# Value and carried products 128 columns wide, in a gated linear attention with a mixture of experts

## The chip, the core and the metric

The kernel runs on one core of a Trainium2 chip. The metric is device time of one execution in microseconds (us); the figure for a kernel is the median of its runs. The engines are named TensorE (PE, matrix products; PEld is its loading of weights), VectorE (DVE), ScalarE (ACT), GpSimd (POOL) and SyncE (SP, which issues transfers). SBUF is the on-chip memory of 128 partitions, PSUM the memory of eight banks that TensorE writes.

## The reference

Two stages follow one another. The first is a recurrent attention over 4 batches, 8 heads, 768 positions and head width 40. A matrix state C and a vector state n are decayed by a forget gate and take in each position's value and key, in a form stabilized by a running maximum m:

```python
for t in range(S):
    m_new = np.maximum(f_gate[:, :, t] + m, i_gate[:, :, t])
    f_stab = np.exp(f_gate[:, :, t] + m - m_new)
    i_stab = np.exp(i_gate[:, :, t] - m_new)
    C = f_stab * C + i_stab * np.einsum('bhd,bhe->bhde', vt, kt)
    n = f_stab * n + i_stab * kt
    h_tilde = np.einsum('bhde,bhe->bhd', C, qt)
    denom = np.maximum(np.abs(np.einsum('bhd,bhd->bh', n, qt)), 1.0)
    y[:, :, t] = sigmoid(o_gate[:, :, t]) * h_tilde / denom
```

The second stage takes the 3072 resulting rows of 320 numbers, picks for each the best of 4 groups and in it the best of 4 experts, and replaces the row by `combined * relu(x @ w1) @ w2` of that expert (320 to 1024 to 320), weighted with the two softmax weights. All numbers are float32.

## The kernel before

The attention is computed in 24 units: 6 chunks of 128 positions, in each of them the 4 batches, one unit for all 8 heads of a batch (`u = 4 * chunk + batch`). Within a chunk the recurrence is a masked product: scores (k by q, line 203, tile `sp`) times decays (outer sums on TensorE, line 176, tile `aw`, exponentials on ScalarE, line 186, tile `ab`), and the product `pt` (line 208) times the values. The values (line 273, tile `av`) have a column of ones beside the 40 of a head, so each head's result is 41 columns wide (`D1`), the last being the denominator. All eight heads lie side by side in one PSUM bank. What earlier chunks carry comes from the state `Cst`: the carried product (line 227, tile `it`, from chunk 1 on), with the even heads in one bank and the odd ones in another, each again 41 wide. The unit's own contribution to the state (line 246) goes to the rest of the second of these banks.

On VectorE and GpSimd a unit is then finished: `carried2` scales the carried part, `norm1` adds it and computes the denominators, `rows` multiplies by the gate (line 290), `rows2` divides (GpSimd up to unit 19), `store` writes the rows to memory and `turn` transposes them on TensorE (line 301) for the routing logits. The gate itself is a tanh on ScalarE for a whole chunk (`gate_o`, line 154).

The order of work is written by hand up to unit 21: each engine executes its instructions in the order in which the code issues them, and waits at the first that isn't ready. `unit(u)` issues, for one unit, scores of u, the finishing steps of u - 1, masked scores and carried product of u, decays of u + 2, turn of u - 1, then values and state of u. Sums of the gates (`gate_sums`) are made for the first 128 positions, for the next 128, and for the remaining 512 in one piece, on VectorE, in steps that `sum_on` issues between units; the steps for the last 512 positions begin after unit 2. From unit 22 on, the scheduler of the language sets the order by readiness and priority. Weight loads and weight splits for the first expert are issued from units 14 to 21.

The experts follow: 16 of them in the order of their number of rows, each with a gather of its rows, a turn, two layers (lines 738 and 759 to 761, with float32 split into two parts; the last three experts use plain float32 in the first layer, line 706) and a scatter.

`busy` (line 119) issues products whose results nobody reads. Eleven of them stand at the kernel's start.

Of the kernel before, what the change touches and what calls it, by code (L numbers as in the profile page):

```python
# [7 lines left out]
F32 = mybir.dt.float32  # L8
# [4 lines left out]
ALU = mybir.AluOpType  # L13
# [5 lines left out]
P = 128  # L19
B, H, S, D = 4, 8, 768, 40  # L20
NCH = S // P
NU = NCH * B
DM = H * D
# [9 lines left out]
D1 = D + 1  # L33
HC = 4 * D1
# [18 lines left out]
def bc(ap, shape):  # L53
    return ap.broadcast_to(list(shape))
# [3 lines left out]
def lstm_moe(ctx: ExitStack, tc: tile.TileContext, gates, qkT, nat, og, wcat, w1, w2, cst, out):  # L58
    nc = tc.nc
    enter = ctx.enter_context  # L60
    mm = nc.tensor.matmul
# [38 lines left out]
    ap_ = att_pool("att", 1)  # L100
# [2 lines left out]
    Apc = ap_.tile([P, S], BF16, name="Apc")  # L103
    sel_b = ap_.tile([P, B * H], BF16, name="sel_b")
    decs = ap_.tile([P, NCH, B * 4], F32, name="decs")
    Cst = ap_.tile([P, B * 4, D1], F32, name="Cst")
    kws = [ap_.tile([P, H * D + 24], F32, name=f"kw{i}") for i in range(2)]
    bcol = ap_.tile([P, NCH, B * H], F32, name="bcol")
    eacol = ap_.tile([P, NCH, B * H], F32, name="eacol")
    wk = att_pool("wk", 2)  # L110
# [42 lines left out]
    def gate_o(c):  # L153
        nc.scalar.activation(sigs[c], sigs[c], AF.Tanh, scale=0.5)
# [33 lines left out]
    def decay(u, r, **kw):  # L188
        aprod(u, r, **kw)
        exps(u, r)  # L190
# [28 lines left out]
    def carried(u):  # L219
        c, b = divmod(u, B)  # L220
        t = st_[u]
        it = t["it"] = ps_a.tile([P, 2, 512], F32, name="it")
        if c > 0:
            for pr in range(4):
                for r in range(2):
                    rs = slice(64 * r, 64 * r + D)
                    mm(it[:, r, pr * D1:(pr + 1) * D1], t["qk"][rs, 1, pr, :], Cst[rs, b * 4 + pr, :], start=True, stop=True)  # L227

    def carried2(u):
        c, b = divmod(u, B)  # L230
        t = st_[u]
        if c > 0:
            num = t["num"] = wk.tile([P, H, D1], F32, name="num")
            nc.vector.tensor_tensor(num.rearrange("p (j r) e -> p r j e", r=2),
                                    t["it"][:, :, 0:HC].rearrange("p r (j e) -> p r j e", e=D1),
                                    bc(eacol[:, c, b * H:(b + 1) * H].rearrange("p (j r o) -> p r j o", r=2, o=1),
                                       (P, 2, 4, D1)), op=ALU.mult)

    def state(u):
        c, b = divmod(u, B)  # L240
        t = st_[u]
        nt = t["nt"]
        if c < NCH - 1:
            for j in range(H):
                pr, r0 = j // 2, 64 * (j % 2)
                mm(t["it"][r0:r0 + 64, 1, HC + pr * D1:HC + (pr + 1) * D1], t["kw"][:, j * D:j * D + 64],  # L246
                   nt[:, j * D1:(j + 1) * D1], start=True, stop=True)
# [18 lines left out]
    def values(u):  # L266
        c, b = divmod(u, B)
        t = st_[u]
        nt = t["nt"]
        av = t["av"] = ps_1.tile([P, 512], F32, name="av")  # L270
        for j in (0, 2, 4, 6, 1, 3, 5, 7):
            o = j * D1
            ins = mm(av[:, o:o + D1], t["pm"][j % 2][:, j // 2, :], nt[:, o:o + D1], start=True, stop=True)  # L273
        rt["av", u] = ins

    def norm1(u):
        num = st_[u]["av"][:, 0:H * D1].rearrange("p (h e) -> p h e", e=D1)
        if u >= B:
            nc.vector.tensor_tensor(num, num, st_[u]["num"], op=ALU.add)  # L279
        st_[u]["num"] = num  # L280
        den = st_[u]["den"] = wk.tile([P, H], F32, name="den")
        nc.vector.tensor_scalar(den, num[:, :, D], -2.0, 2.0, op0=ALU.mult, op1=ALU.max)
        nc.vector.scalar_tensor_tensor(den, num[:, :, D], 2.0, den, op0=ALU.mult, op1=ALU.max)
        nc.vector.reciprocal(den, den)

    def rows(u):
        c, b = divmod(u, B)
        num = st_[u]["num"]
        xn = st_[u]["xn"] = wk.tile([P, H, D], F32, name="xn")
        nc.vector.scalar_tensor_tensor(xn, sigs[c][:, b, :].rearrange("p (h d) -> p h d", d=D), 1.0, num[:, :, 0:D],  # L290
                                       op0=ALU.add, op1=ALU.mult)

    def rows2(u):
        x = wk.tile([P, 3 * P], F32, name="x", bufs=3)
        (nc.gpsimd if u < 20 else nc.vector).tensor_tensor(
            x[:, 0:DM].rearrange("p (h d) -> p h d", d=D), st_[u]["xn"], bc(st_[u]["den"].unsqueeze(2), (P, H, D)), op=ALU.mult)
        st_[u]["x"] = x

    def turned(tp, x, cols=(0, P, 2 * P)):
# [484 lines left out]
    def run(stage, u):  # L784
        if 0 <= u < NU:
            stage(u)
# [9 lines left out]
    xgs, early_loads, early_splits = {}, [], []  # L796
    MANUAL = 22

    def unit(u, more=0):
        run(loads, u + 3)  # L800
        if u == 6:
            first_tokens()
        if u == 9:
            last_rows()
        if u % B == 1 and u // B + 1 < NCH:
            load_o(u // B + 1)
        with ExitStack() as st:
            if u == MANUAL:
                st.enter_context(tc.issue_after(rt["av", u - 1].ins))
            run(scores, u)  # L810
        run(norm1, u - 1)
        run(rows, u - 1)
        run(state2, u - 1)
        run(rows2, u - 1)
        run(store, u - 1)
        run(mask, u + 1)
        run(lambda v: masked(v, 0), u)
        run(lambda v: masked(v, 1), u)
        run(carried, u)
        run(decayed, u)  # L820
        run(carried2, u)
        run(keyw, u + 1)
        run(lambda v: decay(v, 0), u + 2)
        run(turn, u - 1)
        if u % B == 1 and 1 < u < NU:
            logits_back(u // B - 1)
        go_on(9, "A")
        if u == 5:
            first_rows()
        if u > NU - 2:  # L830
            run(logits, u - 2)
        run(values, u)
        run(state, u)
        run(lambda v: decay(v, 1), u + 2)
        if u == 14:
            chores.append([first_experts(), "B"])
        if u == NU - 2:
            chores.append([early_counts(), "B"])
        if u < MANUAL:
            go_on(4 + more, "B")  # L840
        if u % B == 0 and 0 < u < NU:
            logits_of(u // B - 1)
        if u % B == 2 and u // B + 1 < NCH:
            gate_o(u // B + 1)
        for _ in range(1 if u < 20 else 3):
            put_id()
# [57 lines left out]
    with tc.manual_schedule():  # L904
        nc.sync.dma_start(G[:, :, 0:P], gates[:, :, 0:P])
        nc.scalar.dma_start(cs, cst)
        nc.scalar.dma_start(G[:, :, P:], gates[:, :, P:])
        nc.vector.memset(ones_b, 1.0)
        nc.vector.memset(sep, 0.0)
        nc.scalar.activation(sep, sep, AF.Exp)  # L910
        busy(11)
        nc.vector.memset(R_, 1.0)
        nc.vector.memset(R_.rearrange("h (c t) -> h c t", t=P)[:, :, 0:1], 0.0)
        nc.vector.memset(Dl[:, 0:1], 0.0)
        nc.vector.memset(Apc[96:P], 0.0)
        load_qk(0)
        loads(0)
        load_o(0)
        load_qk(1)
        loads(1)  # L920
        loads(2)
        nc.scalar.copy(sel_b, cs[:, C_SEL:C_SEL + B * H])
        nc.scalar.copy(lt_b, cs[:, C_LT:C_LT + P])
        nc.scalar.activation(neg_b, ident, AF.Copy, scale=NEG)
        sums.append(gate_sums(0, P))
        sum_on(9)
        for t in kws:
            nc.gpsimd.memset(t[:, H * D:], 0.0)
        decay(0, 0)
        decay(0, 1, pool=ps_1, tag="lg")  # L930
        scores(0)
        keyw(0)
        masked(0, 0)
        masked(0, 1)
        carried(0)
        carried2(0)
        sums.append(gate_sums(P, 2 * P))
        decay(1, 0)
        values(0)
        state(0)  # L940
        decay(1, 1, pool=ps_1, tag="lg")
        sum_on(3)
        keyw(1)
        gate_o(0)
        decay(2, 0)
        decay(2, 1, pool=ps_1, tag="lg")
        nc.gpsimd.iota(tokid, pattern=[[P, NBLK]], base=0, channel_multiplier=1)
        nc.gpsimd.tensor_copy(keyb, cs[:, C_15E:C_15E + NE])
        nc.gpsimd.tensor_copy(base_b, cs[:, C_BASE:C_BASE + NE])
        nc.gpsimd.memset(ohsum[0], 0.0)  # L950
        loads(3)
        nc.sync.dma_start(wc, wcat)
        unit(1)
        sum_on(9)
        sums.append(gate_sums(2 * P, S))
        for u in range(2, 5):
            unit(u)
            sum_on((0, 0, 3, 2, 9)[u])
# [151 lines left out]
def _lay(inputs):  # L1110
# [12 lines left out]
    def rows(a):  # L1123
        return a.reshape(B, H, NCH, P, D).transpose(2, 0, 3, 1, 4)

    vv = np.concatenate([rows(v), np.ones((NCH, B, P, H, 1), v.dtype)], axis=-1)
    nat = c(np.concatenate([vv.reshape(NCH, B, P, DM + H), rows(k).reshape(NCH, B, P, DM)], axis=-1))
    og = c(rows(o).reshape(NCH * B, P, DM).transpose(1, 0, 2))
    wg, we = inputs['moe_w_group'], inputs['moe_w_expert']
    wcat = np.concatenate([wg, we.transpose(1, 0, 2).reshape(DM, NE)], axis=1)  # L1130
    wcat = np.pad(wcat, ((0, 0), (0, 12)))
# [40 lines left out]
```

## Time and profile before

| what | value |
|---|---|
| median of 3 runs | 511.03 us (509.88 to 511.22) |
| profiled execution | 513.01 us, its span 511.4 us |
| mean granted clock of TensorE over the span | 0.764 |
| granted clock in 60 to 200 us | 0.50 |
| scores of unit 2, 5, 6, 20, 21 begin at | 20.83, 49.30, 59.62, 200.90, 210.78 us |
| first expert's first product | 253.57 us |
| busy: PE, DVE, ACT, POOL | 97%, 56%, 45%, 34% |

The profile is one execution on the chip. The row PEclk tells what share of its full clock TensorE was granted, in 40 equal slices of the span; a row of stretches gives the same as a decimal. Where the first stretches show 1.00 before 7.2 us, no change of the clock has been recorded yet: the durations of the instructions tell the clock there. A float32 product is recorded as two matmuls. A matmul's duration includes the time until its result is out, so the price of one in a row of many is the distance between starts, or busy time by count.

### The profile page before, as it was taken

Reading aid. Unit: us, or ns where it says so; the run is one execution under the profiler, and the core shown is the slowest. Engines: PE = TensorE matmul, PEld = TensorE weight load, DVE = VectorE, ACT = ScalarE, POOL = GpSimd, SP = SyncE. Lnnn points to the kernel's source line nnn. Section 1 sums busy time; section 2 is a strip of 40 time slices with the busy share of each in tenths; the row PEclk is TensorE's granted clock in tenths of the full one; section 3 lists DMA queues with packets and bytes.
Section 4 is the critical chain, followed back from the end, with each engine's and each line's share of the span. In section 5 each row is a group of like instructions: output and inputs, shape, how many; then the busy total and the mean of one; then the engine's idle time right before and its main releaser. Section 6 shows DMA issues by size and latency. Waiting matters only on the chain.

```text
span 511.4 us, 10100 instructions
## 1 busy us (share of the span) xinstructions
PE 497.2 (97%) x3775; PEld 470.9 (92%) x3775; DVE 285.3 (56%) x714; ACT 229.4 (45%) x551; POOL 175.9 (34%) x219
## 2 busy tenths in 40 slices
PE   8899999999999999999799999999999999999995
PEld 5788999999999999989599999999999999999995
DVE  6573543353455455362683848557656677776441
ACT  4733242332243335420435646456755666567431
POOL 1333343344344334241344331442333332342221
PEclk9855555555555555555589999999999999999999
DMA  8944235735337847236257973574876667644500
GB/s 222 284 116 158 89 76 104 212 90 106 125 78 201 239 125 140 55 35 163 49 174 213 389 270 128 182 250 155 283 275 207 247 209 244 238 174 152 196 14 9
DMA packets 29494, 85.39 MB, mean 167 GB/s; under 512 B 12241, under 2 KB 16154, under 8 KB 25860
## 3 DMA queue, kind: packets, MB, share of 16 engines
q1 hardware_dynamic: 24068, 67.63, 44.7%
q0 software_dynamic: 5152, 16.75, 9.4%
q8 instruction: 30, 0.49, 0.4%
q10 hardware_dynamic: 224, 0.35, 0.3%
q14 instruction: 20, 0.16, 0.1%
HBM read 74.95 MB, written 10.62 MB: 167 GB/s over the span
## 4 chain that ended last, share of the span: by engine, by line
PE 89%; issue 5%; ACT 2%; DVE 2%; POOLq 1%; POOL 1%; DVEq 0%
PE psh L738 18%; PE av L273 15%; PE sp L203 9%; PE it L227 6%; PE po L759 5%; PE po L760 5%; PE po L761 5%; PE aw L176 4%; PE it L246 4%; PE tp L301 3%; PE tpm L301 2%; PE busy L123 2%; PE po L765 2%; PE lg L350 1%; PE po L764 1%
## 5 line engine op out<-in xcount | busy, mean ns | idle before, releaser
L186 ACT ACTIVATE ab<-aw,bcol 128x128 f32<-128x128 f32 x192 | 54.6, 372 | 133.5 <-PE aw L176 130.5
L273 PEld LDWEIGHTS av<-nt,pt 128*128 128x128 f32 x384 | 81.7, 321 | 1.8 <-DVE pt L208 1.0
L273 PE MATMUL av<-nt,pt 128*128 128x41 f32 x384 | 81.5, 398 | 0.4 <-DVE pt L208 0.3
L577 POOL DMA_INDIRECT out_dram<-y,ix x34 | 44.5, 1308 | 73.9 <-ACT y L771 60.2
L759 PE MATMUL po<-w2h,hh 128*128 128x320 f32 (+1 forms) x208 | 65.7, 316 | 1.6 <-ACT hh L692 1.6
L573 POOL DMA_INDIRECT xg<-x_d,ix x34 | 36.8, 1083 | 80.7 <-DMA ix<-itab 37.8
L760 PE MATMUL po<-w2l,hh 128*128 128x320 f32 (+1 forms) x208 | 64.2, 309 | 0.0
L761 PE MATMUL po<-w2h,hh 128*128 128x320 f32 (+1 forms) x208 | 64.2, 309 | 0.0
L635 DVE TENSOR_TENSOR w2l<-w2s,w2h 128x640 fp32r<-128x640 f32 x64 | 50.2, 816 | 20.1 <-ACT w2h L633 13.1
L738 PE MATMUL psh<-xhl,w1h 128*128 128x256 f32 (+4 forms) x352 | 60.1, 292 | 0.9 <-DVE xhl L678 0.5
L208 DVE TENSOR_TENSOR pt<-sp,ab 128x512 f32<-128x512 f32 x48 | 31.1, 686 | 42.5 <-PE sp L203 41.6
L738 PEld LDWEIGHTS psh<-xhl,w1h 128*128 128x128 f32 x352 | 50.9, 194 | 1.5 <-DVE xhl L678 0.8
L203 PE MATMUL sp<-qk 40*128 40x128 f32 x384 | 50.4, 427 | 0.0
L695 DVE SCALAR_TENSOR_TENSOR hh<-psh,hh 128x256 fp32r<-128x256 f32 (+2 forms) x104 | 39.6, 412 | 16.4 <-ACT hh L692 15.8
L692 ACT ACTIVATE hh<-psh 128x512 fp32r<-128x512 f32 (+5 forms) x68 | 33.4, 490 | 31.9 <-PE psh L738 23.1
L203 PEld LDWEIGHTS sp<-qk 40*128 40x128 f32 x384 | 42.3, 312 | 5.6 <-issue 4.5
L633 ACT CAST w2h<-w2s 128x640 fp32r<-128x640 f32 x64 | 43.1, 725 | 0.0
L759 PEld LDWEIGHTS po<-w2h,hh 128*128 128x128 f32 (+1 forms) x208 | 38.9, 187 | 1.8 <-ACT hh L692 1.8
L279 DVE TENSOR_TENSOR av<-av,num 128x328 f32<-128x328 f32 x20 | 10.2, 508 | 52.6 <-PE av L273 52.6
L760 PEld LDWEIGHTS po<-w2l,hh 128*128 128x128 f32 (+1 forms) x208 | 38.9, 187 | 0.0
L761 PEld LDWEIGHTS po<-w2h,hh 128*128 128x128 f32 (+1 forms) x208 | 38.8, 187 | 0.0
L635 DVE TENSOR_TENSOR w1l<-w1s,w1h 128x1024 fp32r<-128x1024 f32 x26 | 31.7, 1220 | 12.2 <-ACT w1h L633 9.9
(191 smaller groups left out, 932.9 us busy)
## 6 DMA issues: line engine op xcount, KB each, us to landing
w1s<-in_w_dram SPq DMA_DIRECT2D x12, 1536.0 KB
w2s<-in_w_dram SPq DMA_DIRECT2D x12, 1280.0 KB
qk<-in_qkT_dram SPq DMA_DIRECT2D x48, 192.0 KB
nt<-in_nat_dram SPq DMA_DIRECT2D x24, 324.0 KB
x_d<-x SPq DMA_DIRECT2D x24, 192.0 KB
sig<-in_og_dram SPq DMA_DIRECT2D x6, 640.0 KB
w1s<-in_w_dram SPq DMA_DIRECT2D x4, 768.0 KB
w1s<-in_w_dram POOLq DMA_DIRECT2D x2, 1536.0 KB
```

The source lines that it names most:

```text
L186: rt["exp"] = nc.scalar.activation(st_[u]["ab"][:, r, j, :], aw[:, j, :], AF.Exp, bias=bcol[:, c, i:i + 1])
L203: mm(t["pm"][r][:, pr, :], qk[rs, 0, pr, :], qk[rs, 1, pr, :], start=True, stop=True)
L273: ins = mm(av[:, o:o + D1], t["pm"][j % 2][:, j // 2, :], nt[:, o:o + D1], start=True, stop=True)
L573: return nc.gpsimd.indirect_dma_start(out=o, out_offset=None, in_=src, in_offset=bass.IndirectOffsetOnAxis(ap=idx, axis=0))
L577: return nc.gpsimd.indirect_dma_start(out=out, out_offset=bass.IndirectOffsetOnAxis(ap=idx, axis=0), in_=y, in_offset=None, bounds_check=N ...
L633: nc.scalar.copy(a, src[:, s])
L635: lows.append(lambda: nc.vector.tensor_tensor(o[rows], src[rows, s], a[rows].bitcast(F32), op=ALU.subtract))
L695: nc.vector.scalar_tensor_tensor(hh[:, f:f + per, dst], src[:, :, t], 0.0, hr.bitcast(F32)[:, :, t], op0=ALU.max, op1=ALU.subtract)
L738: ins = mm(ps[:, g * W:(g + 1) * W], w[:, s], x, start=(n == 0), stop=(n == len(todo) - 1))
L759: mm(po[0:m], hh[:, f, t], w2h[:, s], start=st0, stop=False)
L760: mm(po[0:m], hh[:, f, t], w2l[:, s], start=False, stop=False)
L761: ins = mm(po[0:m], hh[:, f, tl], w2h[:, s], start=False, stop=sp0)
```

## The change

The values and carried products move 128 columns where they moved 41. The 87 columns past a head's own are numbers that happen to lie behind them in the same tile, and their results land in the columns of the heads that follow in the bank, which are written afterwards. So that each head's own columns are written after all that spill over them, the heads lie in the bank in the order in which they are computed: the four even ones, then the four odd ones. Tiles, sums and views behind them follow that order: `num` is a tile of 2 x 4 x 41, `xn` is read with the halves exchanged in `rows2`, and the output gate is permuted when inputs are laid out. The state tile is 87 columns longer and is set to zero once, on GpSimd.

At the start three things move: the gate's tanh of chunk 0 ahead of the second half of unit 1's decays, the state of unit 0 behind these decays, and the decays of unit 2 from ahead of `unit(1)` to behind its scores.

```diff
@@ lstm_moe
-    Cst = ap_.tile([P, B * 4, D1], F32, name="Cst")
+    Cflat = ap_.tile([P, B * HC + P - D1], F32, name="Cflat")
+    Cst = Cflat[:, 0:B * HC].rearrange("p (a e) -> p a e", e=D1)
@@ carried
-                    mm(it[:, r, pr * D1:(pr + 1) * D1], t["qk"][rs, 1, pr, :], Cst[rs, b * 4 + pr, :], start=True, stop=True)
+                    o = (b * 4 + pr) * D1
+                    mm(it[:, r, pr * D1:pr * D1 + P], t["qk"][rs, 1, pr, :], Cflat[rs, o:o + P], start=True, stop=True)
@@ values
-        for j in (0, 2, 4, 6, 1, 3, 5, 7):
-            o = j * D1
-            ins = mm(av[:, o:o + D1], t["pm"][j % 2][:, j // 2, :], nt[:, o:o + D1], start=True, stop=True)
+        for r in range(2):
+            for pr in range(4):
+                i, o = (r * 4 + pr) * D1, (2 * pr + r) * D1
+                ins = mm(av[:, i:i + P], t["pm"][r][:, pr, :], nt[:, o:o + P], start=True, stop=True)
@@ rows2
-            x[:, 0:DM].rearrange("p (h d) -> p h d", d=D), st_[u]["xn"], bc(st_[u]["den"].unsqueeze(2), (P, H, D)), op=ALU.mult)
+            x[:, 0:DM].rearrange("p (j r d) -> p r j d", r=2, d=D),
+            st_[u]["xn"].rearrange("p (r j d) -> p r j d", r=2, d=D),
+            bc(st_[u]["den"].rearrange("p (r j o) -> p r j o", r=2, o=1), (P, 2, 4, D)), op=ALU.mult)
@@ unit
             run(scores, u)
+        if first:
+            decay(2, 0)
+            decay(2, 1, pool=ps_1, tag="lg")
         run(norm1, u - 1)
@@ the start
+        nc.gpsimd.memset(Cflat, 0.0)
...
         decay(1, 0)
         values(0)
+        gate_o(0)
+        decay(1, 1, pool=ps_1, tag="lg")
         state(0)
-        decay(1, 1, pool=ps_1, tag="lg")
         sum_on(3)
         keyw(1)
-        gate_o(0)
-        decay(2, 0)
-        decay(2, 1, pool=ps_1, tag="lg")
...
-        unit(1)
+        unit(1, first=True)
@@ _lay
-    og = c(rows(o).reshape(NCH * B, P, DM).transpose(1, 0, 2))
+    og = c(rows(o).reshape(NCH * B, P, H // 2, 2, D).transpose(1, 0, 3, 2, 4).reshape(P, NCH * B, DM))
```

How this moves instructions is seen at two places. The first is ScalarE at the start, from the conversions of constants to the first turned rows (`ab` are exponentials of decays, four to each half of a unit, `sig` is the gate). Before:

```order
L924 ACTIVATE neg_b<-cs 128x128
L186 ACTIVATE ab<-aw,bcol 128x128 x16
L154 ACTIVATE sig<-sig 128x1280
L186 ACTIVATE ab<-aw,bcol 128x128 x8
L307 COPY x<-x 128x64
L186 ACTIVATE ab<-aw,bcol 128x128 x4
L321 COPY xT<-tp 128x384
```

Now:

```order
L932 ACTIVATE neg_b<-cs 128x128
L187 ACTIVATE ab<-aw,bcol 128x128 x12
L155 ACTIVATE sig<-sig 128x1280
L187 ACTIVATE ab<-aw,bcol 128x128 x12
L312 COPY x<-x 128x64
L187 ACTIVATE ab<-aw,bcol 128x128 x4
L326 COPY xT<-tp 128x384
```

The tanh of the gate stands ahead of the four exponentials of the second half of unit 1, where it stood behind them.

The second is TensorE within a unit that has a carried product (unit 6; `qk_91` is the pair of keys and queries of that unit, the decays between the rows are as before and their rows are left out by the dots). Before:

```order
L203 MATMUL sp<-qk_91 128x128 x8
L227 MATMUL it<-Cst,qk_91 128x41 x8
L176 LDWEIGHTS sel_b
L176 MATMUL aw<-Apc,sel_b 128x128
...
L273 MATMUL av<-nt,pt 128x41 x8
L246 MATMUL it<-nt,kw_97 64x41 x8
```

Now:

```order
L204 MATMUL sp<-qk_91 128x128 x8
L229 MATMUL it<-Cflat,qk_91 128x128 x8
L177 LDWEIGHTS sel_b
L177 MATMUL aw<-Apc,sel_b 128x128
...
L276 MATMUL av<-nt,pt 128x128 x8
L248 MATMUL it<-nt,kw_97 64x41 x8
```

The order is the same; the carried and the values products have 128 columns instead of 41, the state's product keeps its 41.

More of the change, by code (lines that the diff above doesn't have):

```diff
@@ L232, in carried2 @@
         if c > 0:
-            num = t["num"] = wk.tile([P, H, D1], F32, name="num")
-            nc.vector.tensor_tensor(num.rearrange("p (j r) e -> p r j e", r=2),
+            num = t["num"] = wk.tile([P, 2, 4, D1], F32, name="num")
+            nc.vector.tensor_tensor(num,
                                     t["it"][:, :, 0:HC].rearrange("p r (j e) -> p r j e", e=D1),
@@ L278, in norm1 @@
         if u >= B:
-            nc.vector.tensor_tensor(num, num, st_[u]["num"], op=ALU.add)
+            nc.vector.tensor_tensor(num, num, st_[u]["num"].rearrange("p r j e -> p (r j) e"), op=ALU.add)
         st_[u]["num"] = num
@@ L287, in rows @@
         c, b = divmod(u, B)
[L288 to L291, printed above, removed]
+        xn = st_[u]["xn"] = wk.tile([P, DM], F32, name="xn")
+        nc.vector.scalar_tensor_tensor(xn.rearrange("p (h d) -> p h d", d=D),
+                                       sigs[c][:, b, :].rearrange("p (h d) -> p h d", d=D), 1.0,
+                                       st_[u]["num"][:, :, 0:D], op0=ALU.add, op1=ALU.mult)
     def rows2(u):
@@ L797, in lstm_moe, with unit @@
     MANUAL = 22
-    def unit(u, more=0):
+    def unit(u, more=0, first=False):
         run(loads, u + 3)
```

## The prediction

> **What bounds the kernel now.** I read the page first (busy shares and the clock row), then busy time by stretches cut where the clock changed, then TensorE's timeline at both clocks, then the groups kept apart by shape.
>
> ```profile
> PE 497.2 (97%) x3775; PEld 470.9 (92%) x3775; DVE 285.3 (56%) x714; ACT 229.4 (45%) x551; POOL 175.9 (34%) x219
> PEclk9855555555555555555589999999999999999999
> ```
>
> TensorE counts as busy all through, but from the third slice to about the twentieth its granted clock is half. That stretch is the attention stage, so the stage is bound by TensorE at half speed. The stretches, with columns as headed:
>
> ```profile
> core 0: us, PE busy (x) PEld busy (x) DVE busy (x) ACT busy (x) POOL busy (x), PEclk, DMA share, GB/s
> 0.41:3.82 3.41, 2.56 (x7) 0.91 (x8) 1.50 (x7) 1.71 (x5) 0.21 (x4) 1.00 0.45 102
> 3.82:7.24 3.42, 3.42 (x13) 1.45 (x12) 2.69 (x9) 0.29 (x2) 1.55 (x5) 1.00 1.01 271
> 10.65:14.06 3.41, 2.65 (x36) 2.20 (x36) 1.91 (x9) 1.16 (x5) 0.00 (x0) 1.00 1.04 237
> 17.48:20.89 3.41, 3.00 (x39) 2.56 (x38) 1.55 (x7) 2.11 (x9) 1.04 (x2) 1.00 1.06 270
> 20.89:24.30 3.41, 3.41 (x27) 3.13 (x26) 2.29 (x7) 1.74 (x10) 1.41 (x2) 0.50 1.03 345
> 60.00:200.00 140.00, 140.00 (x1161) 132.64 (x1161) 66.47 (x206) 48.21 (x155) 55.11 (x83) 0.50 0.53 134
> 210.78:253.57 42.79, 39.93 (x236) 35.47 (x232) 20.27 (x91) 9.66 (x27) 13.04 (x12) 0.50 0.37 79
> 256.41:259.82 3.41, 3.41 (x18) 3.41 (x18) 2.98 (x10) 1.83 (x4) 0.55 (x1) 0.50 0.08 5
> 259.82:263.24 3.42, 3.42 (x31) 3.42 (x31) 1.82 (x4) 1.30 (x3) 1.20 (x3) 1.00 0.79 241
> ```
>
> The clock falls at 20.89 and returns at 259.82, when the first expert's wide products have run for one whole stretch; the half-clock time is 70 stretches of 3.41 us. So 100% "busy" (60 to 200) does not keep the clock up: something finer than this row is counted. TensorE's timeline, full clock above the dots, half below (sp scores, it by L227 carried and by L246 state, aw decays, tp turn, av values; a float32 product is recorded as two matmuls, so 8 products are x16):
>
> ```profile
> 1.26 4.88 PE L123 MATMUL busy<-ones_b 128*128 128x512 bf16 x11 [1.26 <-DVE sep L909]
> 7.73 1.16 PE L203 MATMUL sp<-qk 40*128 40x128 f32 x16
> 8.82 0.39 PE L173 MATMUL aw<-neg_b,lt_b 128*128 128x512 bf16 x1
> 16.72 0.50 PE L301 MATMUL tp<-cs,x 128*128 128x128 f32 x3
> 17.05 1.88 PE L273 MATMUL av<-nt,pt 128*128 128x41 f32 x16
> 18.86 0.67 PE L246 MATMUL it<-nt,kw 128*64 128x41 f32 x16
> 19.46 0.39 PE L173 MATMUL aw<-neg_b,lt_b 128*128 128x512 bf16 x1
> 20.83 2.05 PE L203 MATMUL sp<-qk 40*128 40x128 f32 x16
> ...
> 191.32 2.08 PE L203 MATMUL sp<-qk 40*128 40x128 f32 x16
> 193.19 1.77 PE L227 MATMUL it<-Cst,qk 40*128 40x41 f32 x16
> 194.90 0.61 PE L176 MATMUL aw<-Apc,sel_b 128*128 128x128 bf16 x4
> 195.30 0.85 PE L301 MATMUL tp<-cs,x 128*128 128x128 f32 x3
> 195.94 3.48 PE L273 MATMUL av<-nt,pt 128*128 128x41 f32 x16
> 199.34 1.08 PE L246 MATMUL it<-nt,kw 128*64 128x41 f32 x16
> 200.36 0.61 PE L176 MATMUL aw<-Apc,sel_b 128*128 128x128 bf16 x4
> 200.90 2.08 PE L203 MATMUL sp<-qk 40*128 40x128 f32 x16
> ```
>
> The unit at 191.32 takes 9.58 us with no gap. The values take 3.40 us there (195.94 to 199.34) and 1.81 us at full clock (17.05 to 18.86): half the clock, twice the time.
>
> **What a wide product costs.** Before moves 41 columns; 128 and 160 columns of plain float32 stand in the last experts, at full clock:
>
> ```profile
> L706 PE MATMUL psh<-xhl,w1s 128*128 128x160 f32 x96 | 13.4, 299 | 0.0
> L706 PE MATMUL psh<-xhl,w1s 128*128 128x128 f32 x48 | 5.5, 275 | 0.0
> ```
>
> That is 140 and 115 ns apiece, so 0.8 ns a column: 41 columns move in 33 ns, 128 in about 105. A values matmul takes 1.81 / 16 = 113 ns with its 41 columns, as long as one with 128. The rest is the weights' load, behind which the added 87 columns fit. Price of the wide values: 0 (113 against 115 ns). The carried products run in pairs on two halves of the rows, as the scores do: 1.71 us for 16 with 41 columns (193.19 to 194.90), 1.87 for 16 scores with 128 columns (191.32 to 193.19). Price: 0.16 us in each of 20 units at half clock, 3.2 us in all. The bound from above is that nothing of the 87 columns hides: 0.14 us at half clock for each of 384 values matmuls, 53 us. I take the row that has 128 columns, so 0. From below it is 0 too, since nothing is taken away. The new order within the bank, the sums over it and the permuted gate have the same element counts on VectorE and GpSimd; one memset of 743 columns stands on GpSimd where it waits for the first decays. Both 0.
>
> **What it does to the clock.** Count the share of a 3.41 us stretch in which columns move. In 17.48 to 20.89: 12 of the values matmuls at 33 ns (0.40), 16 of the state's in pairs (0.27), 512 + 4 x 128 bfloat16 columns at half the float32 price (0.43): about 0.32 of the stretch, after which the clock fell. In 10.65 to 14.06, with 9 values, the state's 16 and two such decay blocks, it is about 0.41, and the clock stayed. In 0.41 to 3.82 at most 2.56 of 3.41, 0.75, and no rise; 3.82 to 7.24 had some 0.87 (the eleven 512-column matmuls at 0.44 us until 6.1, then two decay blocks), and a 512-column step is 0.22 us afterwards; 256.41 to 259.82 had 1.0, and it rose. So on this count it closes between 0.32 and 0.41 and opens between 0.75 and 0.87. The half-clock unit before moves columns for about 0.57 of its time and is stuck between the two. With 128 columns the values go from 0.3 to over 0.9: a unit at half clock moves columns for 1.70 + 1.70 (scores, carried) + 3.41 + 0.85 + 0.64 + 0.55 = 8.85 of 9.8 us, 0.90, and near 0.95 in its best stretch; at full clock and 6.3 us, 4.4 / 6.3 = 0.70. It would open, and then not close. This is an estimate, with float32 counted as moving all of its 0.8 ns a column.
>
> The Trainium skill, page "TensorE: Matmul & The Clock Gate", section "What's actually happening", lets recent busyness in windows of 3.4 us release a clock that is otherwise halved. The trace agrees on the window (70 stretches of 3.41 us) and disagrees if busy means the busy row: 100% from 60 to 200 at 0.50. Taken that way the wide columns would leave the clock alone, and the time would be that of the first rival below.
>
> **The start.** Gate's tanh now stands ahead of the second half of unit 1's decays, and scores of unit 1 ahead of unit 2's decays.
>
> ```profile
> 13.91 1.29 ACT L154 ACTIVATE sig<-sig 128x1280 f32<-128x1280 f32 x1
> ...
> 15.23 0.49 DVE L290 SCALAR_TENSOR_TENSOR xn<-sig,av 128x320 f32<-128x320 f32 x1 [2.46 <-ACT sig L154]
> ...
> 24.18 1.26 DVE L853 TENSOR_TENSOR_SCAN M__120<-G,M__120 32x512 f32<-32x512 f32 x1
> 28.75 0.68 DVE L861 TENSOR_TENSOR G<-G,A__122 32x512 f32<-32x512 f32 x1
> 29.86 0.44 DVE L290 SCALAR_TENSOR_TENSOR xn<-sig,av 128x320 f32<-128x320 f32 x1
> ...
> 32.19 3.63 PE L273 MATMUL av<-nt,pt 128*128 128x41 f32 x16
> ```
>
> VectorE stops 2.46 us for the tanh; up to 2.5 us can go, 0 if the gate's transfer is late; I take 1.5. Then a new hole: after unit 2's masked scores VectorE does 5.2 us of gate sums (24.18 to 29.4) before it normalizes. At half clock TensorE worked through that; at full clock its own work there is 1.85 + 0.6 + 0.2 + 1.1 + 0.2 = 4 us and the next turn and values wait some 3 us. With columns moving for a quarter of that stretch the clock probably falls there all the same, some 3 us of work having been won, and is opened again in the units with carried products. I put scores of unit 5 at 45.5 instead of 49.30: -3.8 (0 if it falls as before, -11 if it never falls).
>
> **The units.**
>
> ```profile
> 49.30 1.23 PE L203 MATMUL sp<-qk 40*128 40x128 f32 x8
> 210.78 2.08 PE L203 MATMUL sp<-qk 40*128 40x128 f32 x16
> 253.57 0.58 PE L738 MATMUL psh<-xhl,w1h 128*128 128x256 f32 x1 [0.45 <-ACT xhl L677]
> ```
>
> Units 5 to 20 take 161.5 us, 10.1 each. At full clock TensorE needs 1.09 (scores) + 1.09 (carried) + 1.83 (values) + 0.60 (state) + 0.33 (turn) + 0.44 (decays) = 5.4 us. The other engines do not halve: VectorE has 66.47 / 14 = 4.75 us a unit, ScalarE 3.4, GpSimd 3.9, and the transfers 0.53 of 10.0 us, 5.3 us. All are under 5.4, none by much, and in the chain from values to normalize, rows, masked scores and the next values VectorE has about 3.1 us against 3.6 us of TensorE work in between. I add 0.9 us for what no longer fits (routing, weight splits and early weight loads in units 13 to 20): 6.3 us, with bounds of 5.6 and 7.3. Saving 161.5 - 16 x 6.3 = 60.7 us (72 to 45).
>
> **The tail.** From 210.78 to the first expert product at 253.57 TensorE is busy for 39.93 us, but routing on VectorE (20.27 us) and gathers follow one another there, and the clock may well fall again. Of the 20 us that full clock could save I take 9 (0 to 14), and 1 in the expert's first stretch.
>
> Sum: -3.8 - 60.7 - 9 - 1 = -74.5. The profiled execution took 513.0 us (span 511.4), so 438.5; the median of the runs is 2 lower, 511.03: 437 us.
>
> **The rivals.** (1) The clock stays half. If each float32 column counts for one cycle of its two, the wide unit moves for about 0.5 of its time, short of the 0.75 that did not open the clock, and once it falls in the hole it stays down. For: 0.32 and 0.41 lie close together, and none of the stretches before has dense float32 at half clock. Against: a column does take 0.8 ns throughout. Then +3.2 for the carried products, -1.5 for the start: 512.7 us, the slower side of 511.03, and from the point where less than 1.5 us of the start comes through it is slower by more than 0.3%. (2) It opens late or falls again and again, with stalls as in the hole: half of the 74 us, about 475. (3) The added columns are not hidden behind the loads: 565 us; against it stands the 115 ns row. (4) Transfers bind: 5.3 us a unit is a floor of 0.53 x 161.5 = 86 us for units 5 to 20, so it costs nothing by itself up to 5.4 us a unit; with weights for two experts in the last seven units it costs some us, which lie in the 6.3.
>
> **The numbers.** Opens and mostly holds: 0.62, own range 412 to 462. Late or wavering: 0.13, 462 to 505. Half clock to the end: 0.22, 508 to 517. Not hidden: 0.03. The range 412 to 505 holds some 0.73 of these with the first case's tails cut, so I take it a little into the third, to 511. A difference under 0.3% (1.5 us) can't be told from none. Faster 0.77: the first two cases and a little of the third. Within 0.3%: 0.10 and slower: 0.13, both from the third and fourth.
>
> **What would show it.** The clock row at full tenths between the fifth and the tenth slice, and values at 1.8 us per unit there with 128 columns, prove the clock step; 3.4 us a unit at 0.50 refute it and keep the price. A dip at about 25 us, with TensorE waiting for VectorE after its 512-column scans, proves the hole. Spacing of scores near 6.3 us, with VectorE over 75% busy, proves the unit. I am wrong if the clock stays at 0.50 past 60 us, or if units at full clock take 8 us.

## The result and the profile after

The changed kernel takes 433.01 us (median of 4 runs, 430.04 to 433.8); the kernel before, run beside it, 511.12 us (4 runs, 509.88 to 511.66). The ratio is 0.8464, with a 95% interval of 0.8421 to 0.8507. The forecast was 437 us, with 412 to 511.

One thing is needed to read the numbers further down: in single runs of the kernels with narrow products TensorE's mean granted clock was higher (0.81 to 0.87) than in the profiled one (0.76 to 0.77), so that the kernel before took 482.4 to 485.6 us in 4 of 25 later runs, which the medians count in and against two of which, taken beside it, the changed kernel still comes to 0.892 of the time.

The profiled execution took 433.8 us. The busy shares and the clock row of its page:

```profile
span 432.2 us, 10108 instructions
PE 406.0 (94%) x3775; PEld 382.5 (89%) x3775; DVE 286.0 (66%) x714; ACT 230.8 (53%) x551; POOL 173.3 (40%) x220
PEclk9978899999998987599999999999999999999999
```

Of TensorE's 497.2 busy microseconds 406.0 are left, with the same 3775 matmuls, and the fives of the third to the twentieth slice are gone but for one, in the seventeenth, where the attention has ended. The other engines do what they did, in less time, so their shares rise. Stretches of the changed kernel (busy time of each engine with its count of instructions, the granted clock, the share of the DMA engines, GB/s):

```profile
core 0: us, PE busy (x) PEld busy (x) DVE busy (x) ACT busy (x) POOL busy (x), PEclk, DMA share, GB/s
24.56:27.97 3.41, 2.04 (x32) 1.61 (x28) 3.27 (x7) 2.31 (x5) 0.00 (x0) 1.00 1.00 292
27.97:31.39 3.42, 1.83 (x9) 1.83 (x10) 3.35 (x8) 1.68 (x6) 2.52 (x3) 0.50 0.27 82
31.39:34.80 3.41, 3.41 (x28) 3.12 (x27) 2.42 (x7) 0.00 (x0) 1.08 (x2) 0.50 0.36 107
41.63:45.04 3.41, 2.80 (x41) 2.40 (x40) 2.15 (x5) 1.27 (x6) 1.41 (x2) 1.00 0.74 194
45.04:48.45 3.41, 3.41 (x20) 3.41 (x18) 2.28 (x8) 1.51 (x5) 1.87 (x4) 0.50 0.79 245
50.00:135.00 85.00, 82.04 (x1187) 74.91 (x1185) 66.80 (x212) 50.38 (x159) 54.52 (x83) 1.00 0.91 208
133.78:137.20 3.42, 2.27 (x37) 1.96 (x36) 3.25 (x10) 1.22 (x5) 1.58 (x2) 1.00 1.03 287
137.20:140.61 3.41, 3.41 (x19) 3.41 (x18) 0.33 (x1) 1.51 (x5) 2.75 (x11) 0.50 1.11 233
142.01:177.53 35.52, 26.79 (x237) 22.62 (x233) 22.47 (x93) 10.12 (x29) 12.04 (x12) 0.82 0.50 120
```

From 50 to 135 us the clock is full throughout. Up to unit 20 it falls after 24.56 to 27.97, 41.63 to 45.04 and 133.78 to 137.20, and each time it is back after one or two stretches, in which wide values run: a fall now costs a few microseconds instead of the whole stage. VectorE is busy for 66.80 of 85 us and the transfers take 0.91 of that time; TensorE for 82.04. TensorE's timeline at the start, in units 7 and 20, and at the start of unit 21 and of the first expert:

```profile
20.12 1.16 PE L204 MATMUL sp<-qk 40*128 40x128 f32 x16
...
26.35 0.38 PE L177 MATMUL aw<-Apc,sel_b 128*128 128x128 bf16 x4
29.56 0.90 PE L306 MATMUL tp<-cs,x 128*128 128x128 f32 x3 [2.83 <-POOL x L298]
30.25 3.62 PE L276 MATMUL av<-nt,pt 128*128 128x128 f32 x16
...
41.91 0.72 PE L204 MATMUL sp<-qk 40*128 40x128 f32 x8
...
55.84 1.16 PE L204 MATMUL sp<-qk 40*128 40x128 f32 x16
56.84 1.14 PE L229 MATMUL it<-Cflat,qk 40*128 40x128 f32 x16
57.91 0.40 PE L177 MATMUL aw<-Apc,sel_b 128*128 128x128 bf16 x4
58.14 0.50 PE L306 MATMUL tp<-cs,x 128*128 128x128 f32 x3
58.48 1.95 PE L276 MATMUL av<-nt,pt 128*128 128x128 f32 x16
60.36 0.67 PE L248 MATMUL it<-nt,kw 128*64 128x41 f32 x16
61.28 1.16 PE L204 MATMUL sp<-qk 40*128 40x128 f32 x16
...
135.82 1.16 PE L229 MATMUL it<-Cflat,qk 40*128 40x128 f32 x16 [1.15 <-DVE Cflat L263]
...
142.01 1.16 PE L204 MATMUL sp<-qk 40*128 40x128 f32 x16
...
177.53 0.58 PE L743 MATMUL psh<-xhl,w1h 128*128 128x256 f32 x1 [0.45 <-ACT xhl L682]
```

The unit from 55.84 to 61.28 takes 5.44 us, where the unit before at 191.32 took 9.58. Its sixteen values matmuls take 1.88 us, 117 ns each, with 128 columns; with 41 they took 113.

Where the 79.2 us between the two spans (511.4 and 432.2) came from:

| stretch | before | after | difference |
|---|---|---|---|
| start of the span to scores of unit 5 | 49.30 | 41.91 | -7.4 |
| units 5 to 20 | 161.5 | 100.1 | -61.4 |
| scores of unit 21 to the first expert product | 42.8 | 35.5 | -7.3 |
| the rest | 257.8 | 254.7 | -3.1 |

### The profile page after: what moved, and what is told of

Read it like the earlier page. It is cut to its first block, busy times and chain, and to the rows that moved or that the text cites. A ratio compares the mean times of both kernels' runs of the same rounds, so it can differ in the third digit from the quotient of the medians.

```text
span 432.2 us, 10108 instructions
## 1 busy us (share of the span) xinstructions
PE 406.0 (94%) x3775; PEld 382.5 (89%) x3775; DVE 286.0 (66%) x714; ACT 230.8 (53%) x551; POOL 173.3 (40%) x220
## 4 chain that ended last, share of the span: by engine, by line
PE 71%; issue 11%; DVE 9%; DMA 4%; POOL 2%; POOLq 1%; ACT 1%; DVEq 0%
PE psh L743 21%; PE av L276 6%; PE po L764 6%; PE po L765 6%; PE po L766 6%; PE sp L204 3%; PE it L229 3%; PE tpm L306 3%; DMA sig<-in_og_dram 3%; PE aw L177 2%; PE po L770 2%; PE it L248 2%; PE po L769 2%; PE psh L711 2%; PE tp L306 1%
## 5 line engine op out<-in xcount | busy, mean ns | idle before, releaser
L578 POOL DMA_INDIRECT xg<-x_d,ix x34 | 40.4, 1189 | 81.5 <-DMA ix<-itab 47.4
L582 POOL DMA_INDIRECT out_dram<-y,ix x34 | 39.8, 1170 | 73.4 <-ACT y L776 58.9
L276 PE MATMUL av<-nt,pt 128*128 128x128 f32 x384 | 52.9, 295 | 0.2 <-DVE pt L209 0.2
L276 PEld LDWEIGHTS av<-nt,pt 128*128 128x128 f32 x384 | 50.4, 210 | 1.0 <-DVE pt L209 0.4
L776 ACT ACTIVATE y<-po,xg 128x320 f32<-128x320 f32 (+1 forms) x26 | 13.7, 528 | 45.4 <-PE po L766 40.2
L743 PE MATMUL psh<-xhl,wsk 128*128 128x256 f32 (+4 forms) x176 | 36.5, 289 | 0.0
L743 PE MATMUL psh<-xhl,w1l 128*128 128x256 f32 (+4 forms) x176 | 36.3, 288 | 0.0
```

Source lines behind the costliest of these rows:

```text
L276: ins = mm(av[:, i:i + P], t["pm"][r][:, pr, :], nt[:, o:o + P], start=True, stop=True)
L578: return nc.gpsimd.indirect_dma_start(out=o, out_offset=None, in_=src, in_offset=bass.IndirectOffsetOnAxis(ap=idx, axis=0))
L582: return nc.gpsimd.indirect_dma_start(out=out, out_offset=bass.IndirectOffsetOnAxis(ap=idx, axis=0), in_=y, in_offset=None, bounds_check=N ...
L743: ins = mm(ps[:, g * W:(g + 1) * W], w[:, s], x, start=(n == 0), stop=(n == len(todo) - 1))
```

## Experiments

All kernels compute the whole output. Where `busy` products are added, nobody reads their results. "The count" below is the prediction's: the share of a 3.41 us stretch in which columns move.

**Which of the two products opens the clock.** First the carried products put back to 41 columns, then only the values:

```diff
# values_only
-  mm(it[:, r, pr * D1:pr * D1 + P], t["qk"][rs, 1, pr, :], Cflat[rs, o:o + P], ...)
+  mm(it[:, r, pr * D1:pr * D1 + D1], t["qk"][rs, 1, pr, :], Cflat[rs, o:o + D1], ...)
# carried_only
-  ins = mm(av[:, i:i + P], t["pm"][r][:, pr, :], nt[:, o:o + P], ...)
+  ins = mm(av[:, i:i + D1], t["pm"][r][:, pr, :], nt[:, o:o + D1], ...)
```

> The values move 128 columns, the carried products 41 as before; bank order and start as in the change. Theory A (the clock goes by the share of a 3.41 us stretch in which columns move, weighted by the rows of the array that they use, a float32 column counted for its whole 0.8 ns; it falls below about 0.38 and rises above about 0.8): the values alone fill a stretch at half clock, so the clock reopens; at full clock the unit's share drops by about 0.09, so it falls somewhat more often: 433 to 450 us. Theory B (the same share without the weight by rows): also opens, 433 to 445 us. Theory C (the carried products were needed to open it): about 510 us.

> The carried products move 128 columns, the values 41. Theory A: scores and carried products use 80 of 128 rows, so their 3.7 us in a half-clock unit count for 0.57 and no stretch comes near 0.8: the clock stays at 0.50 to the end of the attention stage, 511 to 515 us (3.2 us more for the carried products, less up to 4 us for the start). Theory B: scores and carried products together are 3.7 us at 0.91 in every half-clock unit, above what opened the clock elsewhere, so it opens: 450 to 490 us, since at full clock the narrow values let it fall again.

Values alone: 436.86 us (434.85 to 439.08), some 4 more than the change, which was not run beside it. Carried alone: 507.58 us (467.53 to 513.54, the other three from 505.62). With wide values the clock opens in all four runs; with wide carried products alone it stays at half in the profiled one from 28.94 to 261.04 us, and two more runs took about as long. Why the run of 467.53 us was shorter, no trace shows. The stretches and the timeline of the kernel with wide carried products only:

```profile
60.00:200.00 140.00, 140.00 (x1143) 130.60 (x1141) 66.13 (x205) 47.06 (x149) 53.59 (x82) 0.50 0.53 131
172.30:175.71 3.41, 3.41 (x31) 3.19 (x30) 1.79 (x3) 0.53 (x4) 0.77 (x2) 0.50 0.82 290
```

```profile
171.03 2.08 PE L204 MATMUL sp<-qk 40*128 40x128 f32 x16
172.90 1.92 PE L229 MATMUL it<-Cflat,qk 40*128 40x128 f32 x16
174.75 0.61 PE L177 MATMUL aw<-Apc,sel_b 128*128 128x128 bf16 x4
175.15 0.85 PE L306 MATMUL tp<-cs,x 128*128 128x128 f32 x3
```

In 172.30 to 175.71 scores, carried products, decays and turn follow one another without a pause: by the prediction's count columns move for 0.97 of it, more than in the 0.87 that opened the clock before, and the clock stays at 0.50. What these products have less of is rows: scores and carried products use 40 of each 64 rows of the array, as `40*128` says. With 40/64 for them the stretch counts (0.60 + 1.85) x 0.625 = 1.53 us of scores and carried products and some 0.9 of decays and turn, 0.71 of 3.41 us. So a count that fits has to be weighted by rows. The values use all 128 rows; by this count that is why they carry the change.

**The new order at the start.** The start alone with both products 41 columns wide, and both wide with the old start:

```diff
# no_start (start_only: both products narrowed as above)
         values(0)
-        gate_o(0)
-        decay(1, 1, pool=ps_1, tag="lg")
         state(0)
+        decay(1, 1, pool=ps_1, tag="lg")
         sum_on(3)
         keyw(1)
+        gate_o(0)
+        decay(2, 0)
+        decay(2, 1, pool=ps_1, tag="lg")
...
-        unit(1, first=True)
+        unit(1)
```

> Both products 41 columns wide; the new order at the start, the bank order and the longer state tile stay. Theory A and B: the clock falls after some 20 to 28 us and stays down: 507 to 511 us, the start being worth 0 to 4 us. A rival in which the order at the start, not the width, keeps the clock: below 480 us.

> Both products 128 columns wide, the order at the start as before the change. Theory A: the clock is reopened by the wide products wherever it falls, so only the start's own gain is missing: 432 to 438 us. A rival in which the start had to keep the clock up until the carried products begin: above 450 us.

The start alone: 511.53 us (506.29 to 513.38), beside 511.1 of the kernel before: nothing. Its clock fell at 28.42 instead of 20.89 us and came back only with the experts, at 257.12. So the bank order, the longer state tile and the start don't make the change; the width does. Without the new start the wide kernel took 430.46 us (429.64 to 432.1), 2.5 less than the change's 433.01, which was not taken beside it. To settle that sign both were run again side by side, as change_again and no_start_again:

> The change itself once more, beside the two below on one chip: 430 to 434 us.

> Both products 128 columns wide, the order at the start as before the change, once more beside the change itself. If the change's start order is worth what the tanh's earlier place was to bring, this is 1 to 2 us slower than the change; if its first measurement (430.5 against 433.0 us) was more than chance, it is 1 to 3 us faster.

The change 431.05 us (6 runs, 429.51 to 431.71), without the new start 431.98 (6 runs, 430.93 to 432.38). The difference has turned round and is 0.9 us: the new start is worth nothing that can be told. Scores of unit 2 begin at 20.12 us with it and at 20.72 without; the 0.6 us doesn't reach the end.

**How wide is wide enough.** Both products with 72 and with 104 columns, which separates a threshold from a gain in proportion (483 and 455 us in proportion):

```diff
-  mm(av[:, i:i + P], ..., nt[:, o:o + P])   # and the carried product alike
+  mm(av[:, i:i + 104], ..., nt[:, o:o + 104])   # the other kernel: 72
```

> Both products 72 columns wide, everything else as in the change. A values matmul then moves columns for 0.56 of its time at any clock (72 of 128). Theory A: the best stretch at half clock (decays, turn and values) reaches about 0.69, under the 0.76 that did not open the clock before the change, so once fallen at about 25 us it stays at 0.50: 508 to 514 us. If the benefit grew in proportion to the columns, 72 would give (72 - 41) / 87 = 0.36 of it: about 483 us.

> Both products 104 columns wide. A values matmul moves columns for 0.81 of its time. Theory A: the best stretch at half clock reaches about 0.86, above the 0.82 that opened the clock, but only where a stretch lies well over the values: it opens, in some units late, and falls a little more often: 432 to 450 us. In proportion to the columns: 0.72 of the benefit, about 455 us.

72 columns: 508.7 us (508.67 to 508.81, one run at 468.51), half clock from 28.66 to 257.35. 104 columns: 434.91 us (431.95 to 438.11), opened at 43.20, full until 138.8. So, leaving aside the one run at 468.51, a threshold lies between: at half clock the weighted count of the 72-column kernel reaches at most 0.72 of a stretch, and in the 104-column kernel the stretch ahead of 43.20 has 0.82.

**Is the width needed to hold the clock, or only to open it?** The narrow kernel, with 18 products of 512 bfloat16 columns issued once, after the values of unit 6:

```diff
         run(values, u)
+        if u == 6:
+            busy(18)
         run(state, u)
```

> Both products 41 columns wide, and 18 unread products of 512 bfloat16 columns once, behind the values of unit 6 (7.7 us at half clock). Theory A: they fill a whole stretch and open the clock there; the narrow unit at full clock has a weighted share of about 0.4 on average, so it falls again within a few stretches and stays down: some 5 us lost, up to 5 gained, 505 to 516 us, with full clock for 3 to 20 us near 60. If opening it once were enough: below 460 us.

It took 475.91 us (5 runs, 475.73 to 493.44), where 505 to 516 were expected, or below 460 if opening once were enough: both missed. Its timeline and stretches:

```profile
67.85 6.40 PE L124 MATMUL busy<-ones_b 128*128 128x512 bf16 x18
...
75.11 1.16 PE L204 MATMUL sp<-qk 40*128 40x128 f32 x16
...
80.32 1.16 PE L204 MATMUL sp<-qk 40*128 40x128 f32 x16
```

```profile
69.19:72.60 3.41, 3.41 (x10) 1.17 (x9) 0.40 (x2) 0.00 (x0) 0.72 (x1) 0.50 0.00 0
72.60:123.80 51.20, 50.30 (x743) 46.46 (x742) 37.89 (x121) 28.82 (x94) 32.89 (x50) 1.00 0.82 185
120.39:123.80 3.41, 2.51 (x39) 2.27 (x36) 3.29 (x10) 2.55 (x7) 2.15 (x3) 1.00 0.59 69
123.80:226.00 102.20, 98.85 (x703) 90.78 (x703) 53.57 (x188) 33.92 (x96) 35.81 (x54) 0.50 0.53 128
```

One dense stretch (69.19 to 72.60) opens the clock, and then narrow units hold it for fifteen stretches, 51.2 us, at 5.21 us a unit (75.11 to 80.32). Their weighted count from 76 to 119 us is 0.39 to 0.53. The stretch from 120.39, in which TensorE paused for 0.9 us, has 0.32; the clock falls after it and narrow units at half clock don't bring it back. So narrow units mostly keep the clock that they find: at full clock they lie just above the count at which it falls, at half clock below the one at which it opens. What the wide kernel has is that its units at half clock open it again, after one to three stretches in the traces taken (three in the last kernel of this section).

**Filling instead of widening.** First the hole of unit 3 in the changed kernel, then the narrow kernel with the same filler and three such products ahead of the turn in units 4 to 21:

```diff
# fill_hole (narrow_filled: products narrowed, and the two lines in comments too)
+        if u == 3:
+            busy(6, ps_1, "lg")
+        # if 3 < u < MANUAL:
+        #     busy(3, ps_1, "tp")
         run(turn, u - 1)
```

> The change as it is, with 6 unread products of 512 bfloat16 columns ahead of the turn in unit 3, where TensorE waited 2.83 us for VectorE's gate sums; they take 1.3 us of that wait. Theory A: the stretch at 24.6 us goes from 0.29 to over 0.5, the clock does not fall at 28 us, and units 3 and 4 run at full clock: 2 to 4 us faster than the change, 429 to 431 us. If the wait itself (any idle time of nearly 3 us) makes the clock fall, it falls all the same and the time stays at 433 us.

> Both products 41 columns wide; 6 unread products of 512 bfloat16 columns in the wait of unit 3, and 3 such ahead of the turn in each unit from 4 to 21 (0.64 us at full clock). Theory A: nothing but the share counts, wherever it comes from. The narrow unit's weighted share at full clock, about 0.42, rises by 0.64 / 6.2 to over 0.5, so the clock does not fall for most of the stage, though nothing reopens it where it does: 430 to 450 us, 470 if it falls once half way. If the width of the products itself were needed: about 515 us.

The hole filled: 429.33 us (427.41 to 430.93), in the expected 429 to 431 and the lowest median of all, but not run beside the change, so the gain of 2 to 4 us isn't settled. TensorE's timeline there:

```profile
26.80 1.46 PE L124 MATMUL busy<-ones_b 128*128 128x512 bf16 x6
29.79 0.55 PE L306 MATMUL tp<-cs,x 128*128 128x128 f32 x3 [1.53 <-POOL x L298]
30.17 1.95 PE L276 MATMUL av<-nt,pt 128*128 128x128 f32 x16
```

The filler takes 1.46 us of the 2.83 us wait, the clock doesn't fall there (it does once in unit 5, at 43.14), and the values at 30.17 take 1.95 us instead of 3.62. The start is as late as it was (29.79 against 29.56): the hole is set by VectorE (its timeline stands in the next section) and not by TensorE's clock.

The narrow kernel with fillers: 495.76 us (488.7 to 522.8) where 430 to 450 were expected, or 470: a miss. Its stretches:

```profile
27.77:31.19 3.42, 1.82 (x17) 1.56 (x15) 3.32 (x10) 1.58 (x6) 2.25 (x3) 1.00 0.74 192
31.19:78.97 47.78, 47.33 (x353) 39.91 (x352) 19.50 (x59) 14.04 (x47) 16.15 (x24) 0.50 0.35 98
78.97:130.17 51.20, 49.27 (x677) 42.63 (x676) 33.16 (x110) 24.90 (x80) 28.17 (x44) 1.00 0.77 171
130.17:200.00 69.83, 68.94 (x516) 58.64 (x515) 30.30 (x88) 24.16 (x71) 24.46 (x43) 0.50 0.55 141
```

It fell behind the hole's filler (count 0.24), three products a unit were too few to open the clock for fourteen stretches, then they did once, and after 130.17 not again. Filler can open a clock; this much of it is not enough to do so reliably, and it takes time at half clock, which the hidden columns don't.

**A version meant to beat the change.** The old start, the hole filled, three fillers at the stretches that still fell (units 5, 15, 18, 20), the gates of later chunks loaded a unit earlier, and two of the subtractions in the 512-position gate sums on GpSimd:

```diff
+        if u == 5: busy(3, ps_1, "tp")           # ahead of scores; in units 15, 18, 20 ahead of carried products
-        if u % B == 1 and u // B + 1 < NCH:
+        if u in (1, 4, 8, 12, 16):
             load_o(...)
-        q = nc.gpsimd if lo == 0 else nc.vector
+        q = nc.vector if lo == P else nc.gpsimd
```

> Both products 128 columns wide, start order as before the change, the unread products in unit 3's wait, 3 more ahead of the scores of unit 5 and ahead of the carried products of units 15, 18 and 20 (where TensorE waited 0.6 to 1.2 us), the gates of chunks 2 to 5 loaded one unit earlier, and half of the 512-column gate sums on GpSimd. Theory A: no fall of the clock between 5 and 145 us and 1.4 us less wait in unit 3: 424 to 428 us. If the falls were not caused by the low shares: 429 to 431 us, the falls being where they were.

434.27 us (6 runs, 431.44 to 436.94), beside 431.05 of the change: a miss, and a little slower. In its trace the clock falls at other places, at 16.48 for 3.4 us and at 43.78 for 10.2; the weighted counts of the stretches ahead are 0.38 and 0.34, so the edits closed some gaps and left others. Which of its edits costs what was not taken apart.

## Why the prediction was right, and where not

The range of the forecast reaches to 511 us, the time of the kernel before, and so says little; what can be judged is the 437 us, the terms of its sum and the mechanism.

**The price of the wide products.** Right. Values cost 117 ns with 128 columns (115 predicted, 113 before). Sixteen carried products take 1.85 us at half clock with 128 columns (172.90 to 174.75) and took 1.71: 0.14 us a unit (0.16 predicted). The third rival (not hidden, 565 us) falls with that.

**The clock.** The conclusion was right, the count only in part. The step that failed is "a unit at half clock moves columns for ... 0.90": it left out rows. By that count the carried-only kernel with 0.97 should have opened the clock, and didn't. With scores and carried products weighted by rows (3.40 x 0.625 instead of 3.40) the 8.85 us become 7.58 and the 0.90 becomes 0.77, no more than the opening point found below: by that alone the clock need not have opened. What opened it are the stretches that lie mostly on the values, which use all rows: the one from 31.39, with wide values from 30.25 to 33.80, has 0.83, those from 45.04 and 137.20 have 1.00 and 0.98. The prediction's "near 0.95 in its best stretch" was the part that held; that the mean it argued from lay too high did no harm, which was luck. "And then not close" failed too: the clock closed twice in units 5 to 20, for one stretch each.

I counted all stretches of 14 traces anew (1896 of them, 110 changes of the clock): columns times the time of one (0.42 ns for bfloat16, from 216 ns between starts of 512 columns in fill_hole, and the same for split products; 0.83, twice as much, for plain float32, of which 32 more columns cost 24 to 27 ns between starts; all doubled at half clock), times the part of the rows and columns of the array in use. One falling point near 0.36 and one opening point near 0.775 then leave 6 stretches on the wrong side (4 to 9, by where in its record a product's columns are placed); without the rows the best two points leave 42, and with a float32 column counted for one cycle of its two 35. The prediction's bounds (0.32 to 0.41, 0.75 to 0.87) hold both points. The points were fitted to these same traces, and a few matmuls are missing from them, so their second digit is an estimate, and another weighting that fits as well is not excluded. Some stretches:

| stretch | clock | weighted count | then |
|---|---|---|---|
| before, 17.48 | 1.00 | 0.33 | fell |
| before, 10.65 | 1.00 | 0.41 | stayed |
| after, 24.56 / 41.63 / 133.78 | 1.00 | 0.29 / 0.36 / 0.36 | fell |
| after, 51.9 to 133.8 | 1.00 | 0.40 to 0.82, mean 0.67 | stayed |
| before, 60 to 200 | 0.50 | 0.35 to 0.66, mean 0.49 | stayed |
| carried_only, 60 to 200 | 0.50 | 0.30 to 0.74, mean 0.55 | stayed |
| after, 31.39 / 137.20 | 0.50 | 0.83 / 0.98 | opened |

The first rival's premise, one cycle of two, is thereby refuted as far as these traces go: the changed kernel's clock opened after a stretch that would count about 0.4 by it (31.39), while half-clock stretches of up to 0.7 did not open it. The Trainium skill, page "TensorE: Matmul & The Clock Gate", section "What's actually happening", lets the clock fall after at least one idle window. The trace agrees on the window (the changes of the clock lie whole numbers of 3.41 us apart) and not on idle: TensorE was busy for 2.04 to 2.80 of the 3.41 us ahead of the three falls quoted above.

**The start: mis-sized.** Predicted -3.8 (45.5 instead of 49.30), measured -7.4. The hole came where it was expected, with the length expected (2.83 against "some 3" us) and behind the gate sums, as VectorE's timeline of the changed kernel shows:

```profile
12.51 0.44 DVE L292 SCALAR_TENSOR_TENSOR xn<-sig,av 128x320 f32<-128x320 f32 x1
...
22.59 1.26 DVE L861 TENSOR_TENSOR_SCAN M__120<-G,M__120 32x512 f32<-32x512 f32 x1
...
27.16 0.68 DVE L869 TENSOR_TENSOR G<-G,A__122 32x512 f32<-32x512 f32 x1
...
28.27 0.43 DVE L292 SCALAR_TENSOR_TENSOR xn<-sig,av 128x320 f32<-128x320 f32 x1
```

What was wrong is "opened again in the units with carried products". The values of unit 3 (30.25) opened it alone, at 34.80, two stretches after the fall and before the first carried product at 36.14, so the time to unit 5 ran mostly at full clock. The tanh step (-1.5) failed as well: VectorE no longer waits for it (12.51, with no wait, against 15.23 with 2.46), but without the whole reordering, where that wait is back (2.53 us in no_start), the kernel takes the same time to within 0.9 us.

**The units.** Right: 161.5 became 100.1 us, 6.26 each (6.3 predicted), -61.4 against -60.7. The 5.4 us of TensorE's own work is the 5.44 of the unit at 55.84. The 0.9 for what no longer fits proved as large (0.82), though not all from the causes named, and in that it was luck. The falls after 41.63 and 133.78 were not among them: unit 5 (41.91 to 50.03) took 8.1 us and unit 20 (133.51 to 142.01) 8.5, the 14 units between 5.96 each. Nor were 3.0 us of waits for the state's update on VectorE:

```profile
PE it L229 <- DVE Cflat L263: 3.0, 5, 1.1
PE aw L177 <- ACT ab L187: 0.7, 1, 0.7
```

(total, count and longest in us, from 40 to 142 us of the changed kernel). That VectorE would be over 75% busy is borne out by 66.80 of 85 us, 79%.

**The tail and the experts.** -7.3 against -9. The clock does fall again there: 0.82 on the mean from 142.01 to 177.53, with TensorE busy for 26.79 of 35.52 us. The experts gave -3.1 against -1: the clock opens 4.0 us behind the first expert product (181.57 against 177.53) where it took 6.3 (259.82 against 253.57), which is about 1 us; the other 2 us I can't assign.

The errors of the terms cancel only in small part: -3.6 at the start, -0.7 in the units, +1.7 in the tail, -2.1 behind it, -4.7 together. The fourth rival, transfers, holds in small part: they take 0.91 of the time from 50 to 135 us, and once TensorE waits 0.73 us for decays (at 84.71) whose exponentials stand behind a tanh that ScalarE began at 82.21, after 2.16 us of waiting for the gate's transfer. The second rival, a clock that wavers, was seen in the narrow kernel with fillers; in the change the falls are there, but short.

## What to carry to other kernels

Read the granted clock beside TensorE's busy share: a busy share of 100% at 0.50 is a stage in which too few columns and rows move, and it can be freed without taking any work out. Where each product loads its own weights, moving columns can hide behind that load (here 128 float32 columns took 117 ns a product against 113 with 41), so a narrow product over all rows can be widened at almost no cost, if its spill is overwritten later; here, widening one that uses 40 of 64 rows did little. Make the loop dense enough to open the clock by itself, then a single gap cost one to three stretches here; the loop that only held it lost it after a stretch with 0.9 us of pause.

## What was not expected of the hardware

The clock has two points with a wide space between: with the rows weighted, in the 14 traces it fell after stretches of at most 0.38 and opened after stretches of at least 0.74. Narrow units lie between them in both states (0.39 to 0.53 at full clock, held for 51.2 us; 0.35 to 0.66 at half clock, held for 140 us and more), so the same narrow instructions run at 5.21 or at 9.58 us a unit depending on what went before.

Rows count: products on 40 of each 64 rows, with the decays and the turn behind them, moved columns for 0.97 of a stretch at half clock without opening it.
